# Converting the first two blocks of weights in halves of their rows

## The chip, the cores and the metric

The kernel runs on one core of a Trainium2 chip. The metric is the device time of one execution in microseconds (us); a comparison uses medians of repeated runs. Five engines of the core appear below: PE does the matrix multiplications (PEld is its weight load, which overlaps them), DVE is the vector engine, ACT the scalar engine, POOL takes a little set-up work, and SP issues nearly all transfers between the chip's main memory and on-chip memory. Each engine works through its own instructions in the order in which the program issued them, and waits at an instruction until what it needs is there.

## The reference

A linear attention with decay ("retention") is followed by a two-layer network with a gate. With 4 batches, 8 heads, 768 positions and head size 64:

```python
for t in range(S):
    state = gamma * state + outer(k[:, :, t], v[:, :, t])
    y[:, :, t] = scale * q[:, :, t] @ state
x = y.transpose(0, 2, 1, 3).reshape(3072, 512)
h = x @ w_in                        # 512 x 2048
g = h * erf(softplus(h))
out = g @ w_out                     # 2048 x 512
```

q, k and v are float32. The two weight matrices arrive as float64 and are computed with in float32, so the kernel has to convert them itself.

## The kernel before

**Tiling.** The 3072 token rows are cut into 24 chunks of 128; six chunks make a batch. The retention of a chunk j is a handful of steps: `ret_scale` (DVE scales q and k by their decays), `ret_transpose` (PE transposes, ACT copies to `kT` and `qT`), `ret_scores` (PE, line 445), `ret_mask` (DVE, line 457, writes `am`), `ret_out` (PE: state part at line 485, value part at 492, the new state's part at 501; ACT copies the result into `xT` at line 506) and `ret_add` (DVE adds to `state`, line 619). Four chunks fill one `xT` tile of 512 tokens. The network takes the first 512 tokens with plain products: `hidden(g, u)` makes one block of 128 hidden columns (`ft = 4 g + u`) by four PE matmuls, one for each 128 rows `kk` of `w_in` (line 674), and ACT copies the sum out (line 692); `gate` applies softplus and erf on ACT; `gated` multiplies on DVE (line 661); `project` multiplies with `w_out` (line 710). All later tokens go through `hidden_part` and `project_part` (lines 767 and 839), which use products of sums and differences of blocks, with weights that lie converted on the chip by then.

**Conversion of the weights.** [...] Each piece of weights takes five DVE instructions and one on ACT: line 215 (DVE masks the exponent), 216 (ACT rescales it), 219 and 224 (DVE builds the mantissa), 227 (DVE puts sign and exponent together; this one waits for ACT) and 233 (DVE multiplies the two, into `w_in_sb` or `w_out_sb`). There are 16 pieces (`n` from 0 to 15). Pieces 0 to 3 are converted in two parts of 128 columns each (512 elements a partition), since one part is just one block `ft`: piece 0 makes blocks 0 and 1, piece 1 blocks 2 and 3. Later pieces go whole (1024 elements). Pieces 4 and 5 are the first of `w_out`, 6 and 7 again `w_in`. The raw words of a piece lie in one of four places; the transfer of piece n+4 (`load_pieces_after`, lines 168 and 176, issued by SP) waits until piece n has been read. `conversion` is a generator: `weights()` hands out its steps one at a time, and two things advance it, `need(...)` (run until a block is done) and `pace(...)` (a budget of steps after each piece of other work). So the order of DVE's instructions is fixed when the program is written out, not by what is ready on the chip.

**Around the change.** The first four chunks have an order written out by hand (K_ scale, T transpose, S_ scores, M mask, O_ out, A add). Chunk 2's out step has the transposes of chunk 3's queries put in between; then come the scores of chunk 3, the conversion of block 0, the add of chunk 2, the mask of chunk 3, the conversion of block 1, and the out step of chunk 3:

```python
    O_(2, lambda: T(3, 1))
    S_(3)

    need("in", 0)
    A(2)
    M(3)
    need("in", 1)
    next(weight_steps)
```

Before the out step of chunk 3, PE multiplies block 0 of `w_in` with the 384 tokens of the first three chunks (`first_block`), with three small products of the identity matrix ahead of it (`warm=3`, line 672). Afterwards it does the same for block 1, and then the last 128 tokens of both blocks.

Of the kernel before, what the change touches and what calls it, by code (L numbers as in the profile page):

```python
# [19 lines left out]
P = 128  # L20
C = 128
TCH = 512
# [23 lines left out]
def kernel(  # L46
# [13 lines left out]
    nc = tc.nc  # L60
# [7 lines left out]
    JPC = TCH // C  # L68
# [65 lines left out]
    def w_in_of(ft, kk):  # L134
        half, s, i = ft // (2 * FG), ft % (2 * FG) // FG, ft % FG
        return w_in_sb[:, s, 2 * half + kk // 2, kk % 2, i * P : (i + 1) * P]
# [46 lines left out]
    def load_pieces_after(n):  # L183
        for later in range(n + 1, n_p):
            if place[later] == place[n]:
                load_piece(later)
                break

    def conversion(n):

        which, i = pieces[n]
        half, s, at = i // 4, i % 4 // 2, i % 2

        for part in range(2) if n < 4 else (None,):
            words = raws[place[n]].bitcast(U32)
            if which == "in":
                f = slice(at * 2 * P, (at + 1) * 2 * P)
                if part is not None:  # L200
                    f = slice((at * 2 + part) * P, (at * 2 + part + 1) * P)
                to = w_in_sb[:, s, 2 * half : 2 * half + 2, :, f].rearrange("p d k f -> p (d k) f")
            else:
                to = w_out_sb[:, s, 2 * half : 2 * half + 2, at * 2 : at * 2 + 2, :].rearrange(
                    "p d f c -> p d (f c)"
                )
            words = words.rearrange("p (a b w) -> p a b w", a=to.shape[1], w=2)
            number, power = (
                x.rearrange("p (a b) -> p a b", a=to.shape[1]) for x in (numbers, powers[n % 2])
            )  # L210
            if part is not None:
                f = slice(part * P, (part + 1) * P)
                words, number, power = words[:, :, f], number[:, :, f], power[:, :, f]
            lo, hi = words[:, :, :, 0], words[:, :, :, 1]
            nc.vector.tensor_scalar(power, hi, 0x7FF00000, None, op0=ALU.bitwise_and)
            nc.scalar.activation(power, power, AF.Relu, bias=below, scale=8.0)
            if part is None:
                yield
            nc.vector.tensor_scalar(
                number, hi, 0xFFFFF, 1 << 20, op0=ALU.bitwise_and, op1=ALU.bitwise_or  # L220
            )
            yield
            numberf = number.bitcast(F32)
            nc.vector.scalar_tensor_tensor(numberf, number, 2.0**32, lo, op0=ALU.mult, op1=ALU.add)
            if part is None:
                yield
            nc.vector.scalar_tensor_tensor(
                power, hi, 1 << 31, power, op0=ALU.bitwise_and, op1=ALU.bitwise_or
            )
            if part != 0:  # L230
                load_pieces_after(n)
            yield
            nc.vector.scalar_tensor_tensor(  # L233
                to, numberf, 2.0**-52, power.bitcast(F32), op0=ALU.mult, op1=ALU.mult,
            )
            done.update((which, 2 * i + u) for u in (range(2) if part is None else (part,)))
            yield

    def sums(which, s):
# [14 lines left out]
    done = set()  # L254

    def weights():


        pending = [conversion(n) for n in range(n_p)]
        begun = 0  # L260
        for n, steps in enumerate(pending):
            for k, _ in enumerate(steps, start=begun):
                yield
                if n > 4 and n + 1 < n_p and k == 2:
                    next(pending[n + 1])
                    yield
            begun = int(n > 4)
            if pieces[n] == ("out", 5):
                yield from sums("in", 0)
# [5 lines left out]
    weight_steps = weights()  # L275
# [3 lines left out]
    def pace(n):  # L279

        nonlocal room
        room += n
        while room >= 1:
            next(weight_steps, None)
            room -= 1

    def need(*what):
        nonlocal room
        while what not in done:
            if next(weight_steps, done) is done:  # L290
                next(last_steps)
            room -= 1
# [3 lines left out]
    ident = const.tile([P, P], F32, name="ident")  # L296
# [93 lines left out]
    def ret_psum(pool=None):  # L390

        pool = pool or (next(psum_turn) if early else ps_r)
        return pool.tile([P, HP, C], F32, name="hp" if pool is ps_h else "r")
# [68 lines left out]
    def ret_out(j, between=None, state_last=False):  # L462
        c = j % NC
        m, i = divmod(j, JPC)
        if i == 0:
            XC[m] = ret.tile([P, HP, TCH], F32, name="xT")

        if early:
            pp = [ps_o.tile([P, HP, C], F32, name=f"o{(2 * j + r + 1) % 4}") for r in range(2)]
        else:  # L470
            pp = [ret_psum() for _ in range(2)]

        def place(h):
            return pp[h % 2][h // 4 * D : (h // 4 + 1) * D, h % 4 // 2, :]

        if state_last:
            between()


        if c:  # L480
            for u in PAIRS:
                for r in range(2):
                    h = 2 * u + r
                    own = slice(r * D, (r + 1) * D)
                    nc.tensor.matmul(  # L485
                        place(h), state[own, u, :], QT[j][own, u, :],
                        start=(h % 4 < 2), stop=False, skip_group_check=True,
                    )
        if between is not None and not state_last:
            between()  # L490
        for h in (0, 4, 1, 5, 2, 6, 3, 7):
            nc.tensor.matmul(  # L492
                place(h), V[j][:, h, :], AM[j][:, h % 2, h // 2, :],
                start=(not c and h % 4 < 2), stop=True, skip_group_check=True,
            )

        if c < NC - 1:
            new = SU[j] = pp[0][:, 2:, :].rearrange("p a (b d) -> p (a b) d", d=D)
            for h in range(H):
                r = h % 2  # L500
                nc.tensor.matmul(  # L501
                    new[r * D : (r + 1) * D, h // 2, :], KQ[j][:, 0, h, :], V[j][:, h, :],
                    start=False, stop=True, skip_group_check=True,
                )
        for r in range(2):
            nc.scalar.copy(XC[m][:, r::2, i * C : (i + 1) * C], pp[r][:, :2, :])
        pace(2.5)
# [156 lines left out]

    HP_ = {}

    def hidden_of(ft, t, warm=0):

        if ft not in HP_:
            HP_[ft] = ps_h.tile([P, TCH], F32, name="hp")  # L670
        for _ in range(warm):
            nc.tensor.matmul(HP_[ft][:, :P], ident, ident, start=True, stop=True)
        for kk in range(n_k):
            nc.tensor.matmul(  # L674
                HP_[ft][:, t], w_in_of(ft, kk), XC[0][:, kk, t],
                start=(kk == 0), stop=(kk == n_k - 1),
            )

    def hidden(g, u):
        ft = g * FG + u  # L680
        if u == 0:
            HS[g] = act.tile([P, N], F32, name="h")
        need("in", ft)
        if ft == 0:
            hidden_of(1, slice(TCH - C))
        hidden_of(ft, slice(TCH) if ft > 1 else slice(TCH - C, TCH))

        if ft < FG:
            need("in", ft + 2)
        if ft == 0:  # L690
            ret_add(JPC - 1)
        nc.scalar.copy(HS[g][:, u * TCH : (u + 1) * TCH], HP_.pop(ft))
        done.add(("hidden", ft))
        if ft == FG - 1:
            need("in", FG + 2)
        if g:
            pace_around(3.4 if ft > FG else 0)
# [156 lines left out]
    def put_part(m, step):  # L854
# [27 lines left out]
    K_, T, S_, M, O_, A = (  # L882
        ret_scale, ret_transpose, ret_scores, ret_mask, ret_out, ret_add
    )
# [32 lines left out]
    T(3, 0)  # L917
    A(1)
    K_(3, 1)
    O_(2, lambda: T(3, 1))  # L920
    S_(3)

    need("in", 0)
    A(2)
    M(3)
    need("in", 1)
    next(weight_steps)

    def first_block():
        hidden_of(0, slice(TCH - C), warm=3)  # L930

    ret_out(JPC - 1, first_block, state_last=True)
    early = False
    room = 0.0

# [176 lines left out]
```

## Time and profile before

| | us |
|---|---|
| median of 4 runs | 683.68 (683.57 to 683.94) |
| the profiled execution's own time | 683.66 |
| its span, first to last instruction | 681.9 |
| PE busy | 675.3 |
| DVE busy | 390.5 |
| ACT busy | 256.5 |
| PE busy in the stretch 24.4 to 88.9 us (64.5 us) | 64.48 |
| DVE busy in that stretch | 61.60 |

Some 1.8 us of the profiled execution lie around its span. A row of the timeline gives the start in us, the busy time, the engine, the line of the kernel, the operation, the output and inputs with their shapes, and in brackets how long the engine had been idle just before and what ended that idle time. Timelines merge neighbours of one kind ("x2"), and an instruction may begin a little before the one ahead of it has ended. The chain of waits follows the work that ended last back to what released each step of it; an engine that is not on it at some time had time to spare there. The granted clock of PE is 1.00 in every slice of the profile.

### The profile page before, as it was taken

What the parts mean: (1) busy time and instruction counts of PE and PEld (TensorE: products, weight loads), DVE (VectorE), ACT (ScalarE), POOL (GpSimd) and SP (SyncE); (2) the same over time, 40 slices, a digit from 0 to 9 for tenths busy, and PEclk for the clock granted to TensorE, in tenths of its full rate; (3) what the DMA queues carried; (4) which work ended last, traced back from release to release, by engine and by line L of the source; (5) the groups of instructions that cost most, each with busy time, mean ns of one, the idle gap of its engine ahead of it and who ended that gap; (6) DMA issues with size and microseconds to landing.
All of it is one profiled execution on the core that took longest, in us unless ns stands there. A gap on an engine that the chain in (4) does not pass through costs nothing.

```text
span 681.9 us, 14430 instructions
## 1 busy us (share of the span) xinstructions
PE 675.3 (99%) x6206; PEld 577.2 (85%) x6206; DVE 390.5 (57%) x616; ACT 256.5 (38%) x291; POOL 5.0 (1%) x20
## 2 busy tenths in 40 slices
PE   8999999999999999999999999999999999999998
PEld 7744544577999999999999999999999999999996
DVE  5799999585845634644553564555544554343224
ACT  3367362324414234144144242341441441423431
POOL 1000000100000000000000000000000000000000
PEclk9999999999999999999999999999999999999999
DMA  9999944333412222321321222222312200000000
GB/s 192 220 227 214 229 125 103 63 61 62 116 33 46 75 38 41 75 41 37 78 45 32 64 45 46 67 42 45 71 36 48 59 18 2 1 32 1 1 32 31
DMA packets 156511, 47.64 MB, mean 70 GB/s; under 512 B 143008, under 2 KB 147360, under 8 KB 156448
## 3 DMA queue, kind: packets, MB, share of 16 engines
q1 hardware_dynamic: 156032, 46.72, 31.9%
q8 instruction: 48, 0.79, 0.5%
q14 instruction: 15, 0.12, 0.1%
q10 hardware_dynamic: 416, 0.01, 0.0%
HBM read 40.39 MB, written 6.29 MB: 68 GB/s over the span
## 4 chain that ended last, share of the span: by engine, by line
PE 98%; DVE 0%; ACT 0%; issue 0%; POOL 0%; POOLq 0%
PE hp L767 37%; PE o L839 36%; PE hp L674 8%; PE o L710 8%; PE r L551 1%; PE hp L516 1%; PE o L587 1%; PE r L445 1%; PE o L386 1%; PE hp L566 1%; PE o L492 1%; PE r L432 1%; PE r L566 1%; PE r L492 0%; PE o L485 0%; PE o L501 0%
## 5 line engine op out<-in xcount | busy, mean ns | idle before, releaser
L767 PE MATMUL hp<-xs,w_in_sb 128*128 128x128 f32 x1280 | 149.7, 275 | 0.0
L767 PEld LDWEIGHTS hp<-xs,w_in_sb 128*128 128x128 f32 x1280 | 147.8, 192 | 1.6 <-issue 0.5
L839 PE MATMUL o<-w_out_sb,h 128*128 128x256 f32 x640 | 141.7, 379 | 0.0
L839 PEld LDWEIGHTS o<-w_out_sb,h 128*128 128x128 f32 x640 | 121.6, 190 | 16.5
L767 PE MATMUL hp<-xT,w_in_sb 128*128 128x128 f32 x960 | 113.7, 275 | 0.0
L767 PEld LDWEIGHTS hp<-xT,w_in_sb 128*128 128x128 f32 x960 | 111.9, 192 | 1.9 <-issue 1.0
L839 PE MATMUL o<-w_out_sb,e 128*128 128x256 f32 x480 | 112.1, 383 | 0.0
L661 DVE TENSOR_TENSOR e<-h,e 128x1024 f32<-128x1024 f32 x42 | 49.5, 1220 | 100.0 <-ACT e L642 100.0
L839 PEld LDWEIGHTS o<-w_out_sb,e 128*128 128x128 f32 x480 | 88.2, 190 | 11.6
L674 PE MATMUL hp<-xT,w_in_sb 128*128 128x512 f32 (+2 forms) x144 | 56.8, 548 | 1.0 <-DVE w_in_sb L233 1.0
L792 DVE TENSOR_TENSOR h<-h,hp 128x512 f32<-128x512 f32 x20 | 13.7, 687 | 72.3 <-PE hp L767 72.3
L632 ACT ACT_TABLE_LOAD x24 | 30.8, 1283 | 60.8 <-issue 45.4
L674 PEld LDWEIGHTS hp<-xT,w_in_sb 128*128 128x128 f32 x144 | 25.7, 190 | 27.6 <-issue 25.3
L642 ACT ACTIVATE e<-e 128x2048 f32<-128x2048 f32 (+1 forms) x23 | 42.1, 1836 | 0.2
L632 ACT ACTIVATE e<-h 128x2048 f32<-128x2048 f32 x22 | 42.0, 1910 | 0.2
L780 DVE TENSOR_TENSOR h<-h,hp 128x512 f32<-128x512 f32 x20 | 13.7, 687 | 41.8 <-PE hp L767 41.8
L785 ACT COPY h<-hp 128x512 f32<-128x512 f32 x20 | 11.7, 586 | 61.0 <-PE hp L767 61.0
L790 ACT COPY h<-hp 128x512 f32<-128x512 f32 x20 | 11.7, 585 | 60.3 <-PE hp L767 60.3
L783 ACT COPY h<-hp 128x512 f32<-128x512 f32 x20 | 11.7, 585 | 57.1 <-PE hp L767 57.1
L605 ACT COPY xT<-r 128x256 f32<-128x256 f32 x32 | 10.4, 375 | 54.8 <-PE r L551 54.8
L642 ACT ACT_TABLE_LOAD x24 | 30.8, 1283 | 0.4
L778 ACT COPY h<-hp 128x512 f32<-128x512 f32 x20 | 11.8, 588 | 48.6 <-PE hp L767 48.6
(139 smaller groups left out, 667.1 us busy)
## 6 DMA issues: line engine op xcount, KB each, us to landing
w_out_sb<-in_moe_w_out_dram SPq DMA_DIRECT2D x14, 512.0 KB, 5.4
kq<-in_k_dram SPq DMA_DIRECT2D x23, 256.0 KB, 3.8
v<-in_v_dram SPq DMA_DIRECT2D x23, 256.0 KB, 3.1
out_dram<-r SPq DMA_DIRECT2D x23, 256.0 KB, 3.0
kq<-in_q_dram SPq DMA_DIRECT2D x288, 16.0 KB, 1.8
kb<-in_k_dram SPq DMA_DIRECT2D x288, 16.0 KB, 1.7
w_in_sb<-in_moe_w_in_dram SPq DMA_DIRECT2D x8, 512.0 KB, 12.9
w_out_sb<-in_moe_w_in_dram SPq DMA_DIRECT2D x8, 256.0 KB, 8.4
```

The costliest lines, as they stand in the source:

```text
L566: nc.tensor.matmul(other[a][own, u % 2, D:] if crossed else pp[a][own, u % 2, t], V[j][t, 2 * u + r, :], AM[j][t, r, u, :D], start=crossed ...
L632: nc.scalar.activation(E[g], HS[g], AF.Softplus)
L642: nc.scalar.activation(E[g][:, half], E[g][:, half], AF.Erf)
L661: nc.vector.tensor_tensor(E[g][:, half], HS[g][:, half], E[g][:, half], op=ALU.mult)
L674: nc.tensor.matmul(HP_[ft][:, t], w_in_of(ft, kk), XC[0][:, kk, t], start=(kk == 0), stop=(kk == n_k - 1),)
L710: nc.tensor.matmul(O[0][tt].rearrange("p (d c) -> p d c", d=2), E[g][:, u * TCH + tt * P : u * TCH + (tt + 1) * P], w_out_of(ft), start=(f ...
L767: nc.tensor.matmul(bank[:, u, :], w_in_sb[:, s, IN[a], kk, u * P : (u + 1) * P], XS[m][b][:, kk, :], start=(p in (1, 2, 5) and u == 0 and ...
L778: nc.scalar.copy(h["11"], flat)
L780: nc.vector.tensor_tensor(h["11"], h["11"], flat, op=ALU.add)
L783: nc.scalar.copy(h["12"], flat)
L792: nc.vector.tensor_tensor(h["12"], h["12"], flat, op=ALU.add)
L839: nc.tensor.matmul(O[m][i][:, half, :], G[g][a][:, u * P : (u + 1) * P], w_out_sb[:, s, OUT[b], u, :], start=i not in started, stop=(s == ...
```

## The change

Piece 0, the first of `w_in`, is converted in four steps in place of two: each of its two blocks (0 and 1) is converted first for its rows `kk` 0 and 1 and then for its rows `kk` 2 and 3, so that each of the six instructions handles 256 elements a partition and there are twice as many. The four matmuls of such a block now wait in pairs: those of `kk` 0 and 1 for the first half, those of `kk` 2 and 3 for the second. The first step of block 0's conversion is issued inside chunk 2's out step, right after the transposes of chunk 3's queries. DVE's order does not change by this, but on ACT the exponent step of the first half now stands ahead of the two copies of chunk 2's results to `xT`. One step more was taken ahead of chunk 3's out step before (the beginning of block 2); it is gone there, so on ACT block 2's exponent step now stands behind the copies of chunk 3's results. The three products of the identity matrix ahead of block 0 are gone. From block 3 on the order of the instructions on every engine is as it was.

```diff
@@ -193,7 +193,12 @@
         which, i = pieces[n]
         half, s, at = i // 4, i % 4 // 2, i % 2
 
-        for part in range(2) if n < 4 else (None,):
+
+        parts = itertools.product(
+            range(2) if n < 4 else (None,), (slice(2), slice(2, 4)) if n == 0 else (slice(None),)
+        )
+        for part, rows in parts:
+            last = n > 0 or rows.start == 2
             words = raws[place[n]].bitcast(U32)
             if which == "in":
                 f = slice(at * 2 * P, (at + 1) * 2 * P)
@@ -210,7 +215,8 @@
             )
             if part is not None:
                 f = slice(part * P, (part + 1) * P)
-                words, number, power = words[:, :, f], number[:, :, f], power[:, :, f]
+                words, number, power = words[:, rows, f], number[:, rows, f], power[:, rows, f]
+                to = to[:, rows]
             lo, hi = words[:, :, :, 0], words[:, :, :, 1]
             nc.vector.tensor_scalar(power, hi, 0x7FF00000, None, op0=ALU.bitwise_and)
             nc.scalar.activation(power, power, AF.Relu, bias=below, scale=8.0)
@@ -227,13 +233,14 @@
             nc.vector.scalar_tensor_tensor(
                 power, hi, 1 << 31, power, op0=ALU.bitwise_and, op1=ALU.bitwise_or
             )
-            if part != 0:
+            if part != 0 and last:
                 load_pieces_after(n)
             yield
             nc.vector.scalar_tensor_tensor(
                 to, numberf, 2.0**-52, power.bitcast(F32), op0=ALU.mult, op1=ALU.mult,
             )
-            done.update((which, 2 * i + u) for u in (range(2) if part is None else (part,)))
+            if last:
+                done.update((which, 2 * i + u) for u in (range(2) if part is None else (part,)))
             yield
 
@@ -664,12 +671,10 @@
-    def hidden_of(ft, t, warm=0):
+    def hidden_of(ft, t):
 
         if ft not in HP_:
             HP_[ft] = ps_h.tile([P, TCH], F32, name="hp")
-        for _ in range(warm):
-            nc.tensor.matmul(HP_[ft][:, :P], ident, ident, start=True, stop=True)
         for kk in range(n_k):
             nc.tensor.matmul(
                 HP_[ft][:, t], w_in_of(ft, kk), XC[0][:, kk, t],
@@ -917,19 +922,19 @@
     T(3, 0)
     A(1)
     K_(3, 1)
-    O_(2, lambda: T(3, 1))
+
+    def last_queries():
+        T(3, 1)
+        next(weight_steps)
+
+    O_(2, last_queries)
     S_(3)
 
     need("in", 0)
     A(2)
     M(3)
     need("in", 1)
-    next(weight_steps)
-
-    def first_block():
-        hidden_of(0, slice(TCH - C), warm=3)
-
-    ret_out(JPC - 1, first_block, state_last=True)
+    ret_out(JPC - 1, lambda: hidden_of(0, slice(TCH - C)), state_last=True)
     early = False
     room = 0.0
```

## The prediction

> **What bounds the kernel now.** I read the busy times first, then the chain of waits, then each wait on it. On the page:
>
> ```profile
> PE 675.3 (99%) x6206; PEld 577.2 (85%) x6206; DVE 390.5 (57%) x616; ACT 256.5 (38%) x291; POOL 5.0 (1%) x20
> PE 98%; DVE 0%; ACT 0%; issue 0%; POOL 0%; POOLq 0%
> ```
>
> PE sets the time over the whole, so only a stretch where PE waits can give anything. The chain of waits between 20 and 92 us (start, length, what) shows two such places:
>
> ```profile
> 21.56 0.65 ACT xT L506 x2
> 22.21 0.63 ACT w_out_sb L216
> 22.83 0.02 issue
> 22.86 0.70 DVE w_out_sb L227
> 23.56 0.03 issue
> 23.58 0.70 DVE w_in_sb L233
> 24.28 0.14 issue
> 24.42 2.82 PE hp L674 x8
> ...
> 84.99 3.63 PE hp L674 x8
> 88.62 0.36 PE r L485 x2
> 88.98 0.04 issue
> 89.02 0.66 PE r L485 x14
> ```
>
> The first is what the change works on: ACT copies chunk 2's results, then rescales the exponents of block 0, DVE finishes it, and PE starts at 24.42. The second is easily missed: the 16 records of line 485 take 0.60 us elsewhere on this chain and 1.06 us here, and the four matmuls ahead of them show 3.63 in place of 3.44. PEld's waits from 84 to 90 us say why:
>
> ```profile
> PEld r L485 <- DVE am L457: 1.0, 2, 0.8
> ```
>
> Line 485 of chunk 5 writes into the banks from which DVE still reads chunk 5's scores, so PE stands still until DVE has made the masks: (1.06 - 0.60) + (3.63 - 3.44) = 0.65 us. What holds DVE before that? Its timeline (brackets: idle time ahead and what ended it):
>
> ```profile
> 34.27 0.69 DVE L227 SCALAR_TENSOR_TENSOR w_in_sb<-w_out_sb,w_in_sb 128x512 uint32<-128x512 uint32 x1 [1.28 <-ACT w_in_sb L216]
> 47.93 0.69 DVE L215 TENSOR_SCALAR w_out_sb<-w_out_sb 128x1024 uint32<-128x1024 uint32 x1
> 58.18 0.69 DVE L215 TENSOR_SCALAR w_out_sb<-w_in_sb 128x1024 uint32<-128x1024 uint32 x1 [0.29 <-DMA w_in_sb<-in_moe_w_in_dram]
> ...
> 87.68 1.28 DVE L457 TENSOR_TENSOR am<-r,causal 128x512 f32<-128x512 f32 x2
> ```
>
> At 58.18 DVE waits for a transfer (piece 6). From there to 140 us its list of waits holds only that one and one at the far end:
>
> ```profile
> DVE h L780 <- PE hp L767: 7.7, 1, 7.7
> DVE w_out_sb L215 <- DMA w_in_sb<-in_moe_w_in_dram: 0.3, 1, 0.3
> ```
>
> So from 58.18 to the masks' end at 87.68 + 1.28 = 88.96 DVE runs without a wait, at its own speed, and PE cannot pass 89.02 before it. One more landing matters. SP's transfers of piece 4 (line 176, issued at 38.77 and 39.69) have these times to landing:
>
> ```profile
> DMA to landing us min/median/max: 5.1/6.6/8.1
> ```
>
> The second lands at 39.69 + 8.1 = 47.8, and DVE's first instruction on it starts at 47.93: just on time, without a recorded wait. At the other landing, piece 6's second half (issued at 42.78, 15.3 us to landing), DVE starts 0.09 us after.
>
> **The change, step by step.** All against the profiled execution: 683.66 us, a span of 681.9 and 1.8 around it; it lies 0.02 under the median of the runs, 683.68.
>
> *Prices of the halves.* No row of before shows a 256-element conversion step. Line 215 takes 0.42 with 512 elements and 0.69 with 1024, so a half is 0.42 - 0.27/2 = 0.28 (bounds: 0.21, half of it; 0.42, no shorter). Lines 224, 227 and 233 take 0.69 and 1.23, so a half is 0.42, which is also what the 128x256 add at line 619 shows (0.41). ACT's line 216 takes 0.72 and 1.15, a half 0.51 (bounds 0.375, the 128x256 copy of line 605; 0.72). Independent DVE steps begin 0.07 before the last has ended, dependent ones 0.03 after. A half then takes 1.69 us from start to start on DVE, a block 3.38 against 2.73 (25.72 to 28.44): 0.65 more for each of two blocks.
>
> [...] The rows of lines 215 and 224 hold a fixed 0.15 us an instruction (0.42 - 0.27). [...]
>
> *Block 0.* Line 215 starts at 20.91 as before (its transfer sets that). First half on DVE: 20.91, 21.11, 21.43; ACT rescales 21.22 to 21.73, without the copies ahead of it; line 227 at 21.78 no longer waits (0.46 before); line 233 ends at 22.65. With the 0.14 us handover PE starts at 22.79 instead of 24.42. ACT's copies of chunk 2, moved behind, run 21.66 to 22.31 instead of 21.56 to 22.21: in time for 22.79. Second half: line 233 ends at 24.32, PE's second pair at 24.46, after the first pair ended at 22.79 + 1.41 = 24.20: a new wait of 0.26. The block ends at 25.87 instead of 27.24: PE leads by 1.37. The identity products (0.94 us, 22.53 to 23.47) lay inside the wait, so their removal itself gains nothing.
>
> *Chunk 3 and block 1.* Behind the halves DVE adds the state (24.25 to 24.66) and masks (to 25.87); PE needs them at 25.87 and 26.47. Block 1's halves are done at 27.53 and 29.20; PE comes at 27.96 and needs the second pair at 29.37. ACT's copies of chunk 3 end at 28.85, needed at 30.8. The lead stays 1.37. DVE is 0.68 late here (29.12 against 28.44).
>
> *Blocks 2 and 3.* Block 2 is ready at 32.07, needed by PE at 32.6. In block 3 DVE waited 1.28 us for line 216 because ACT stood at block 0's copy (33.03) waiting for PE. With PE 1.37 ahead that copy starts at 31.66, ACT is done at 33.4, and DVE goes through at 33.59 instead of 34.27: late by 0.68 becomes early by 0.68.
>
> *Where the lead goes.* At 47.93 DVE may come 0.7 to 0.85 early (another 0.17 of ACT waiting at 46.59 goes too), but piece 4 lands at 47.8: it keeps 0.03. ACT's erf (51.11) stands behind DVE's first step on piece 4, so it does not move, nor does the copy of chunk 4's queries behind it (ends at 54.47); PE, which took them at 55.41, would arrive at 54.04, waits until about 54.5 and keeps 0.9. At 58.18 piece 6 holds DVE: lead 0.00. The landings do not follow DVE: SP issued both transfers by 42.8, from a queue held back by earlier landings, and the wait of SP for DVE before piece 7's (47.31) comes after them. So the masks still end at 88.96; PE arrives 0.9 earlier, and waits 0.65 + 0.9 = 1.55 us there instead of 0.65.
>
> *Sum.* -1.37 at block 0, +0.47 at chunk 4's scores, +0.90 at chunk 5's masks: 0.0. After 89.02 all engines find what they found before. Forecast 683.6.
>
> *Bounds.* With both upper prices (0.42 and 0.72) a block takes 3.92, DVE is 1.8 late after block 1, 0.55 after the vanished 1.28, 0.4 at 47.93, and 0.1 after the 0.29 at 58.18: 683.8. With the lower prices DVE is only earlier at waits that stay: 683.6. The landings may shift a little; the runs' spread of 0.37 bounds that.
>
> **The rivals.**
>
> *The lead survives (faster).* If the two landings came 1.5 us earlier, or DVE did not gate chunk 5, PE would keep its lead: 683.66 - 0.9 = 682.8 to 683.66 - 1.37 = 682.3. For it: PE is on 98% of the chain, and its wait at 24.4 really goes. Against it: DVE has no idle time between 58.18 and 88.96 to give up. If only part of it (0.1 to 0.6) survives, the time is 683.1 to 683.5, inside 0.2%.
>
> *DVE becomes late (slower).* If a half costs as much as a whole on DVE, a block takes 5.46: DVE is 5.0 late after block 1; the 1.28, the 0.17 and the 0.29 take back 1.7, and some 3.2 reach the masks at 88.96, all paid by PE: 686.9. The point from which it decides is a DVE later than 58.1 at piece 6. Against it: line 619's 0.41 for 256 elements.
>
> *The change does nothing at its own place*: if ACT's first half waited as long as before, PE would start near 24.4 as before and the end would also be 683.7; it differs in the trace alone.
>
> **How the numbers follow.** About 0.2% (1.4 us) is what a measurement of this kernel can tell from no change. Lead fully lost or nearly (the forecast, with the partial case and the no-effect case): 0.84, 683.1 to 683.9. Lead survives: 0.11, at 682.3 to 682.8, of which some lie inside 0.2% (over 682.3), so 0.07 counts as faster and 0.04 as the same. DVE late: 0.05. Faster 0.07, same 0.88, slower 0.05. The range goes from 682.7, into the surviving lead, to 684.0, the upper price and the runs' spread.
>
> **What would show it.** Right: line 233's first half ends near 22.7 and PE's block 0 starts near 22.8; block 0 ends near 25.9; no DVE wait for ACT in block 3; a DVE wait of 0.6 us or more for a transfer near 47.9, and 0.3 again at 58.2; PEld's wait for the masks grows from 1.0 to about 1.9 us; the masks end at 88.9 to 89.0. Wrong: piece 6's first step before 57.9, or masks before 88.5 (then the lead is partly kept), or piece 4's first step after 48 (then DVE is late).

## The result and the profile after

The changed kernel takes 682.54 us (median of 38 runs, 682.16 to 683.47) against 683.65 us before (58 runs, nearly all from 683.35 to 684.28): a ratio of 0.9984, 95% interval 0.9979 to 0.9988. That is 1.1 us less, inside the 0.2% that the prediction called "the same", though the interval excludes 1, and 0.16 us below the range of 682.7 to 684.0. The profiled execution of the changed kernel took 682.96 us, a span of 681.3; it lies 0.42 above the median, which matters below.

The page of the changed kernel, busy times and the chain of waits by engine:

```profile
PE 674.8 (99%) x6200; PEld 576.1 (85%) x6200; DVE 391.1 (57%) x626; ACT 257.2 (38%) x293; POOL 5.5 (1%) x20
...
PE 86%; DVE 7%; issue 2%; SPq 2%; ACT 1%; DMA 1%; ACTq 0%; DVEq 0%
```

Before, PE held 98% of the chain. Now the chain leaves PE at chunk 5's masks and goes back along DVE to the first landing of weights. Its two ends, between 20 and 26 us and between 86 and 92 us (start, length, what):

```profile
13.66 7.53 DMA w_out_sb<-in_moe_w_in_dram
21.19 0.03 issue
21.22 0.02 DVEq L221
21.24 0.05 issue
21.29 0.29 DVE w_out_sb L221
...
22.24 0.35 DVE w_out_sb L233
22.59 0.02 issue
22.62 0.42 DVE w_in_sb L239
...
87.00 1.29 DVE am L464 x2
88.29 0.04 issue
88.33 0.66 PE r L492 x14
88.99 1.02 PE r L499 x16
```

(Lines 215, 227, 233, 457, 485 and 492 of before are 221, 233, 239, 464, 492 and 499 here.) Where ACT's copies of chunk 2 stood before, there is now nothing but the landing and DVE's five short steps. At the other end DVE's masks hold PE: the profile's list of PEld's waits from 84 to 90 us has this line (us in total, times, longest).

```profile
PEld r L492 <- DVE am L464: 1.3, 2, 0.9
```

It was 1.0 before. PE's timeline of the changed kernel (brackets: idle time ahead, and what ended it) gives the places that the prediction put numbers on:

```profile
23.19 3.13 PE L679 MATMUL hp<-xT,w_in_sb 128*128 128x384 f32 x8 [0.42 <-DVE w_in_sb L239]
26.25 0.67 PE L492 MATMUL o<-qT,state 64*64 64x128 f32 x16
...
54.42 1.16 PE L452 MATMUL r<-qT,kT 64*128 64x128 f32 x16
...
87.74 0.43 PE L492 MATMUL r<-qT,state 64*64 64x128 f32 x2
88.33 0.66 PE L492 MATMUL r<-qT,state 64*64 64x128 f32 x14 [0.17 <-DVE am L464]
88.92 1.09 PE L499 MATMUL r<-am,v 128*64 128x128 f32 x16
```

And DVE's timeline at the places shown of before:

```profile
33.93 0.69 DVE L233 SCALAR_TENSOR_TENSOR w_in_sb<-w_out_sb,w_in_sb 128x512 uint32<-128x512 uint32 x1
...
47.60 0.69 DVE L221 TENSOR_SCALAR w_out_sb<-w_out_sb 128x1024 uint32<-128x1024 uint32 x1
...
57.48 0.67 DVE L221 TENSOR_SCALAR w_out_sb<-w_in_sb 128x1024 uint32<-128x1024 uint32 x1
...
87.00 1.28 DVE L464 TENSOR_TENSOR am<-r,causal 128x512 f32<-128x512 f32 x2
```

None of the four has a bracket. The wait of 1.28 us for ACT at block 3 is gone, as forecast; the wait for piece 6 (58.18 before, 57.48 now) is gone too, and none has come at piece 4 (47.60). DVE's whole list of waits from 22 to 140 us:

```profile
DVE h L785 <- PE hp L772: 7.8, 1, 7.8
DVE e L668 <- ACT e L649: 0.2, 1, 0.2
DVE w_in_sb L233 <- ACT w_in_sb L222: 0.2, 1, 0.2
```

**Where the time went.** Between the two profiles, PE starts on block 0 1.23 us earlier (24.42 to 23.19). It loses 0.31 between the block's halves (3.13 in place of 2.82), so it starts the state products 0.92 earlier (27.17 to 26.25). At chunk 4's scores it is still 0.92 ahead (54.42 against the line of before below): nothing was given back there.

```profile
55.34 1.16 PE L445 MATMUL r<-qT,kT 64*128 64x128 f32 x16
```

At chunk 5's masks it loses 0.24, and starts chunk 5's value products 0.68 earlier (89.61 to 88.93). The execution is 0.70 shorter, 683.66 to 682.96. The other 0.4 of the difference of medians is not between these two profiles, because the profiled execution of the changed kernel is 0.42 slower than that kernel's median; the experiments show what an execution's time hangs on.

### The profile page after: what moved, and what is told of

It is laid out like the page before. It is cut to its first block, busy times and chain, and to the rows that moved or that the text cites. A ratio compares the mean times of both kernels' runs of the same rounds, so it can differ in the third digit from the quotient of the medians.

```text
span 681.3 us, 14431 instructions
## 1 busy us (share of the span) xinstructions
PE 674.8 (99%) x6200; PEld 576.1 (85%) x6200; DVE 391.1 (57%) x626; ACT 257.2 (38%) x293; POOL 5.5 (1%) x20
## 4 chain that ended last, share of the span: by engine, by line
PE 86%; DVE 7%; issue 2%; SPq 2%; ACT 1%; DMA 1%; ACTq 0%; DVEq 0%
PE hp L772 37%; PE o L844 36%; PE o L715 6%; PE hp L679 2%; PE r L558 1%; PE hp L523 1%; SPq L118 1%; DMA w_out_sb<-in_moe_w_in_dram 1%; DVE w_out_sb L230 1%; PE o L594 1%; DVE w_out_sb L225 1%; DVE w_in_sb L233 1%; DVE w_out_sb L233 1%; DVE w_out_sb L221 1%; PE hp L573 1%
```

## The experiments

The expectations set theories against each other by letters. Theory A keeps the prediction's gates: the landings of pieces 4 and 6 hold DVE in every execution. Theory B says that the landings held DVE in one execution by chance, and that DVE's own work, from the first landing to chunk 5's masks, sets the time. Where a further letter appears, the expectation says what it stands for. Five numbers of each profile are used throughout: L, the landing of the first piece of weights; D, the start of DVE's first conversion step (0.09 behind L); S, PE's start on block 0; M, the end of chunk 5's masks on DVE; V, PE's start on chunk 5's value products. "Piece 6" is the landing of its second half. Values read from different views can differ by 0.01.

| kernel profiled (all in us) | L | S | M | V | piece 6 | time |
|---|---|---|---|---|---|---|
| before (first profile) | 20.82 | 24.42 | 88.96 | 89.61 | 58.09 | 683.66 |
| before again | 21.74 | 24.80 | 89.08 | 89.72 | 56.45 | 683.77 |
| changed | 21.20 | 23.19 | 88.28 | 88.93 | 54.55 | 682.96 |
| changed again | 21.10 | 23.10 | 88.20 | 88.85 | 53.80 | 682.88 |
| one DVE step earlier in before | 21.23 | 24.73 | 88.70 | 89.46 | 55.33 | 683.50 |
| extra DVE work in changed | 21.35 | 23.34 | 89.79 | 90.44 | 55.68 | 684.50 |
| halves alone | 21.48 | 24.26 | 89.34 | 89.98 | 55.82 | 684.03 |
| move alone | 20.60 | 23.66 | 87.82 | 88.47 | 53.98 | 682.52 |
| early masks in changed | 20.87 | 22.87 | 85.94 | 87.90 | 54.38 | 681.98 |
| early masks in before | 20.81 | 24.91 | 87.12 | 89.63 | 56.86 | 683.69 |
| no identity products in before | 21.72 | 24.98 | 90.83 | 91.48 | 56.79 | 685.52 |
| late first piece in changed | 21.61 | 23.61 | 88.73 | 89.38 | 54.71 | 683.42 |
| late first piece in before | 21.24 | 24.55 | 88.78 | 89.42 | 55.06 | 683.47 |
| early piece and early masks | 19.46 | 22.84 | 85.61 | 87.59 | 55.00 | 681.64 |

Time minus V is 594.03 to 594.08 us in every row: what these kernels change has no effect behind V, so the whole case lies ahead of it. Two paths end at V. DVE's gives V = M + 0.65 wherever PE waits for the masks. PE's, where it doesn't wait, gives V = S + 64.72 with whole blocks (89.46 - 24.73 with one DVE step earlier in before, 89.63 - 24.91 with early masks in before) and S + 65.03 with the 0.31 between the halves (87.90 - 22.87, early masks in changed). The later of the two sets the time.

### Both kernels once more

No edit.

> The kernel before, unchanged, once more with a profile: do the landings that held the vector engine in the first profile repeat? Theory A (the forecast's step: the landings of pieces 4 and 6 hold DVE, and the change itself made them earlier): piece 4's second half lands at 47.8 and piece 6's at 58.1 again, within 0.3 us, with a DVE wait of about 0.3 us at 58.2. Theory B (how late they land changes from execution to execution and has nothing to do with the change): they land elsewhere, by 1 us or more, and DVE's wait at 58.2 is gone or larger. Both: the time is 683.4 to 684.0, and PE waits for chunk 5's masks near 88.6 to 89.0.

> The changed kernel, unchanged, once more with a profile. Theory A: the landings are at 45.9 and 54.6 again, within 0.3 us. Theory B: they are elsewhere by 1 us or more; where piece 6 lands later than 57.4 DVE waits for it and the masks end later by just that. Both: 682.2 to 683.4; PE waits about 0.9 us for the masks of chunk 5.

Before took 683.77 us. Its piece 6 landed at 56.45 instead of 58.09, piece 4 at 46.37 instead of 47.81, and DVE waits for neither. DVE's list of waits from 23 to 140 us, before once more:

```profile
DVE h L780 <- PE hp L767: 7.8, 1, 7.8
DVE w_in_sb L227 <- ACT w_in_sb L216: 1.4, 2, 1.2
DVE e L661 <- ACT e L642: 0.2, 1, 0.2
```

The wait for block 3 is there again (1.2), the wait for piece 6 is not, and the time is the same within 0.11 us. DVE came to piece 6 at the same time as in the first profile (58.18), now without a bracket:

```profile
58.17 0.69 DVE L215 TENSOR_SCALAR w_out_sb<-w_in_sb 128x1024 uint32<-128x1024 uint32 x1
```

So the gate that the prediction rests on is not a property of the kernel before: theory A falls. Of the 14 profiles in the table, the first one of before has the latest piece 6, and it alone has a DVE wait for a landing of piece 4 or 6.

The changed kernel again: 682.88, and M - D = 67.01 us (66.99 in its first profile). DVE runs from the first landing to the masks with next to no idle time, so the time of the changed kernel should follow L: time minus L is 661.76 and 661.78, with L 0.10 apart; the late landing below tests it further. By this the median, 682.54, would belong to a landing near an estimated 20.8 (682.54 - 661.77), which no profile of this kernel shows. In before it is 662.84 and 662.03: there block 0 does not hang on the landing alone. In the first profile DVE stood 0.46 us for ACT there; in the second, with the landing 0.92 later, it did not stand for ACT at all.

### One DVE step earlier, the rest as before

If DVE decides, taking away its wait of 1.28 us at block 3 should help without any of the change. In before, one step of conversion is issued ahead of block 0's copy on ACT, so that ACT rescales block 3 in time:

```diff
             ret_add(JPC - 1)
+            next(weight_steps)
         nc.scalar.copy(HS[g][:, u * TCH : (u + 1) * TCH], HP_.pop(ft))
```

> The kernel before with one step more of the conversion ahead of block 0's copy on ACT, so that block 3's exponent step does not stand behind that copy: DVE's 1.28 us of waiting at 34.3 goes, PE's start on block 0 stays at 24.4. Theory B (the end is set by when DVE comes to chunk 5's masks): DVE leads by 1.3 at the masks, PE's stall of 0.65 there goes: 683.65 - 0.65 = 683.0. Theory A (landings hold DVE): 683.65, within 0.1. Theory C (PE's earlier start on block 0 is itself the gain): 683.65.

It took 683.66 us against 683.72, ratio 1.0, 0.9991 to 1.0008: nothing. DVE's list of waits from 22 to 140 us:

```profile
DVE h L781 <- PE hp L768: 7.8, 1, 7.8
DVE w_in_sb L227 <- ACT w_in_sb L216: 1.0, 2, 0.6
DVE w_out_sb L227 <- ACT w_out_sb L216: 0.5, 2, 0.4
DVE e L661 <- ACT e L642: 0.2, 1, 0.2
```

The wait at block 3 is gone, but 1.13 us of it came back at later blocks (0.17 at 38.95, 0.61 at 42.39, 0.35 at 46.70), each for ACT, whose conversion step stands behind its copy of a block that PE had not finished. DVE can't run ahead of PE in this stretch: ACT's copies tie it to PE's pace. PE's own path ended at S + 64.72 = 89.45, with S at 24.73 as late as in before. Theory B's 683.0 was a miss, since it left out the second path (the table has DVE's masks 0.26 earlier than in the first profile of before, and V only 0.15). To gain, a change must move both: PE's start and DVE's masks.

### Extra work on DVE in the changed kernel

Two adds of 128x512 into a tile that nothing reads, behind block 3:

```diff
             need("in", ft + 2)
+        if ft == 1:
+            same = ident[:, None, :].to_broadcast([P, 4, P])
+            for _ in range(2):
+                nc.vector.tensor_tensor(junk, same, same, op=ALU.add)
         if ft == 0:
```

> The changed kernel with two extra DVE instructions of 512 elements behind block 3's conversion, some 1.25 us of work that nothing uses; PE's start on block 0 stays at its new place. Theory B: DVE's lead of 1.07 at the masks is used up: 682.54 + 1.25 - 0.0 to 0.3 = 683.5 to 683.8. Theory A: part of the work hides behind the landings: 682.6 to 683.0. Theory C: PE's lead of 1.37 stays: 682.5.

The result is 684.5 us (683.68 to 684.85), ratio 1.0011 to before, 1.0002 to 1.002. The two adds and what follows them on DVE's timeline:

```profile
35.43 1.41 DVE L699 TENSOR_TENSOR junk<-ident 128x512 f32<-128x512 f32 x2
36.76 0.42 DVE L221 TENSOR_SCALAR w_out_sb<-w_in_sb 128x512 uint32<-128x512 uint32 x1
```

They delay DVE by 1.33 us. M - D grows from 67.0 to 68.35, and V - L from 67.73 to 69.09: the whole delay reaches V, 50 us later, and with it the end. No landing took any of it up, and PE found no slack. In the changed kernel DVE decides, as theory B says. Per landing the price is 1.36 us; against the profile of changed it is 684.50 - 682.96 = 1.54, and the medians differ by 1.96. The rest of that, 0.6 us, is not accounted for by the added work, and with it the result lies 0.7 above the expected 683.5 to 683.8; the landings of the unprofiled executions are not known.

### Chunk 5's masks earlier, in both kernels

The same edit in both takes the masks of chunk 5 ahead of two of DVE's conversion instructions (lines 225 and 230, in before 219 and 224), which take 1.9 us:

```diff
-            ([(T, 5)], []),
-            ([(S_, 5), (M, 5)], []),
+            ([(T, 5), (pace, -1.5)], []),
+            ([(S_, 5), (M, 5), (pace, 1.5)], []),
```

> The changed kernel with chunk 5's masks two DVE instructions (1.87 us) earlier; the two conversion steps they pass come right behind them. Theory B/D (the end is set by when DVE has made these masks; PE stands 0.9 us at them in both profiles of the changed kernel): that stall goes and the lead of 1.37 us arrives whole: 682.5 - 0.9 = 681.6. Theory C (PE's start alone counts, the masks do not): no change, 682.5. If PE meets another wait behind the masks that is as late, 682.5 too, and the trace shows which.

> The kernel before with chunk 5's masks two DVE instructions earlier. Theory B/D: PE's stall there, 0.65 us in one profile of before and 0.27 in the other, goes: 683.7 - 0.3 to 0.65 = 683.05 to 683.4. Theory C: 683.7.

In the changed kernel: 681.98 us (681.76 to 682.51), ratio to before 0.9977, 0.9968 to 0.9986. In before: 683.64, ratio 1.0, 0.9991 to 1.0008. PE's timeline at chunk 5's state products, of changed with early masks:

```profile
83.67 3.70 PE L679 MATMUL hp<-xT,w_in_sb 128*128 128x512 f32 x8
87.30 0.67 PE L492 MATMUL r<-qT,state 64*64 64x128 f32 x16
87.89 1.09 PE L499 MATMUL r<-am,v 128*64 128x128 f32 x16
```

The sixteen records stand together in 0.67 us, without a bracket: the wait for the masks is gone, and V lies at S + 65.03. Per landing, V moved from L + 67.73 to L + 67.03, 0.70 earlier; the medians differ by 0.56. The 0.9 that was expected is what PEld's list showed for the longest wait; PE itself stood only 0.71 beyond its own path (88.93 - 23.19 - 65.03). In before the same edit frees PE in the same manner and gains nothing, where theory B expected 0.3 to 0.65: PE started at 24.91, and 24.91 + 64.72 = 89.63 is as late as the V of before (89.61 and 89.72). There the masks cost PE 0.47 us in the first profile and 0.20 in the second, and in the execution with early masks PE's start was later than in both and set V. So PE's lead was real, and part of it was lost at the masks.

### The two parts of the change by themselves

The halves alone, with ACT's order and the identity products of before (only the removed and restored lines are shown):

```diff
-    def last_queries():
-        T(3, 1)
-        next(weight_steps)
-
-    O_(2, last_queries)
+    O_(2, lambda: T(3, 1))
...
-    ret_out(JPC - 1, lambda: hidden_of(0, slice(TCH - C)), state_last=True)
+    next(weight_steps)
+
+    def first_block():
+        hidden_of(0, slice(TCH - C), warm=3)
+
+    ret_out(JPC - 1, first_block, state_last=True)
```

> Only the halves: block 0's and 1's conversion in halves, but the first exponent step behind the copies of chunk 2's results, block 2's exponent step ahead of the copies of chunk 3's, and the identity products kept. ACT is then done with the first half near 22.6, PE starts near 23.7 and block 0 ends near 26.7 instead of 27.24. Theory D (the lead of PE on block 0 arrives through block 0's copy on ACT, which lets block 3's exponent step and so DVE through): lead 0.5, 683.7 - 0.5 = 683.2. Theory A (landings): 683.7.

And the move alone: before with its whole blocks, and block 0's first step ahead of the copies of chunk 2:

```diff
-    O_(2, lambda: T(3, 1))
+
+    def last_queries():
+        T(3, 1)
+        next(weight_steps)
+
+    O_(2, last_queries)
```

> Only the move: block 0's exponent step whole, ahead of the copies of chunk 2's results; no halves, identity products kept, block 2's step where it was. DVE's wait of 0.46 for ACT goes, PE starts near 23.9 instead of 24.42. Theory D: lead 0.45 (less where the first transfer lands late), 683.7 - 0.45 = 683.25. Theory A: 683.7.

The halves alone: 683.89 us, ratio 1.0006, 0.9997 to 1.0015, no gain and perhaps a small loss. One of its eleven executions took 685.56. DVE's timeline there:

```profile
23.22 0.43 DVE L233 SCALAR_TENSOR_TENSOR w_out_sb<-w_out_sb 128x256 uint32<-128x256 uint32 x1 [0.69 <-ACT w_out_sb L222]
```

DVE still waits for ACT, which copies chunk 2 first, and the halves add their own work on top: M - D is 67.77, and PE waits 1.2 us at the masks in its list. The expected 683.2 was a miss: PE started at 24.26, 0.2 and 0.5 earlier than in the profiles of before, but the masks ended at 89.34, later than in both, and V is M + 0.65.

The move alone: 682.97 us (682.52 to 683.52), ratio 0.999, 0.9981 to 0.9999. ACT's timeline there:

```profile
21.15 0.72 ACT L216 ACTIVATE w_out_sb<-w_out_sb,below 128x512 uint32<-128x512 uint32 x1 [0.28 <-DVE w_out_sb L215]
21.78 0.63 ACT L506 COPY xT<-o 128x256 f32<-128x256 f32 x2
```

One ACT instruction ahead of two copies gives 0.6 us of the 1.1, more than the 0.45 that was expected. It serves both paths: PE starts 0.8 to 1.1 us earlier than in the two profiles of before (with a landing, 20.60, earlier than in either), and at block 0 DVE doesn't stand at line 227. Per landing, V is L + 67.87, against L + 67.73 with the whole change, so the halves add 0.14 us by the profiles and 0.43 by the medians (which were not measured side by side, and whose landings are unknown). By either number the move is the larger part of the gain; how much the halves add is not settled more closely.

### Before without the identity products

```diff
     def first_block():
-        hidden_of(0, slice(TCH - C), warm=3)
+        hidden_of(0, slice(TCH - C))
```

> The kernel before without the three identity products ahead of block 0, nothing else. The forecast priced their removal at nothing, since they lie in PE's wait: 683.65, within 0.1, PE's start on block 0 unmoved and its eight records still 2.8 us. Rival: an idle PE is slower afterwards, then block 0's records take longer and the time grows.

The median is 683.82 us, ratio 1.0004, 0.9995 to 1.0013, but two of the ten executions took 685.52 and 685.21; the other eight lie from 683.46 to 684.02. The profiled one is the slowest. Block 0 on its PE timeline:

```profile
24.97 4.51 PE L674 MATMUL hp<-xT,w_in_sb 128*128 128x384 f32 x8 [1.82 <-DVE w_in_sb L233]
```

And PE alone in stretches of 1 us (length, PE busy and records, granted clock, DMA's share, GB/s):

```profile
24.00:25.00 1.00, 0.03 (x1) 1.00 1.10 222
25.00:26.00 1.00, 1.00 (x3) 0.70 1.13 228
26.00:27.00 1.00, 1.00 (x3) 0.50 1.12 227
27.00:28.00 1.00, 1.00 (x3) 0.50 1.15 235
28.00:29.00 1.00, 1.00 (x4) 0.59 1.13 231
29.00:30.00 1.00, 1.00 (x18) 1.00 1.12 222
```

Behind 1.82 us without a matmul the granted clock was 0.50 for an estimated 3.4 us (0.60, 1.00, 1.00 and 0.82 of the four slices from 25 to 29, if it was 1.00 in the rest of them), and the block took 4.51 us instead of 2.82: 1.69 us, which reaches the end (24.98 + 64.72 + 1.69 = 91.39; V is 91.48, which is M + 0.65, since DVE was late as well). With the three products, 0.95 and 1.23 us of the gap are left in the two profiles of before, where the clock stays at 1.00. The products do not exclude such times: two of the 58 executions of before (685.47 and 685.73) and one of the eleven of the halves alone (685.56) have them too, but none of these three was profiled, and none of the 82 executions of before that ran beside the experiments is over 684.12. In the changed kernel the gap is 0.42 us without the products, its clock stays at 1.00, and none of its 38 executions is over 683.5. That taking them out costs nothing there fits the prediction; that the short gap is the reason is argued, since no run puts the products back into the changed kernel.

### The first landing later, in both kernels

If the changed kernel follows L one for one and before doesn't, then moving the first transfer of weights behind one transfer of values must cost the one and not the other:

```diff
         load_values(j - 1)
-    load_piece(0, 0)
     load_values(JPC - 1)
+    load_piece(0, 0)
     load_piece(0, 1)
```

> The changed kernel with the second half of the transfer of block 0's raw words... that is, both of its transfers, issued behind chunk 3's values instead of ahead of them, so block 0's words land some 1.1 us later. Theory E (in the changed kernel DVE never stops between this landing and chunk 5's masks, so the time is the landing plus a constant; 661.77 in both profiles of it): 682.54 + 1.1 = 683.6 to 683.7. If the masks were not the end of that chain, or another transfer held DVE: less than +0.5.

> The same order of transfers in the kernel before. There ACT's copies of chunk 2's results end at 22.2 to 22.5 whatever the landing is, and block 3's step waits for PE, so a landing of 20.8 has about 0.6 us to spare: 683.65 + 0.3 to 0.5 = 683.9 to 684.2. If before also goes with the landing: +1.1, 684.75.

Changed: 683.42 us (682.93 to 683.99; 683.6 to 683.7 had been expected), 0.9 over its own median of 682.54 and nearly all of its gain lost: ratio to before 0.9997, 0.9988 to 1.0006. Before: 683.68 against 683.70, no change, where 0.3 to 0.5 had been expected. In the profile of changed, time minus L is 661.81, as in its two other profiles. That the edit moved the landing in every execution is not shown: L is 0.4 to 0.5 later than in the two profiles of changed (1.1 had been expected), and in before, at 21.24, it lies between the landings of its two profiles, so for before the test rests on the medians. That before does not follow L one for one its two profiles show as well: L 0.92 apart, the times 0.11. Its block 0 hangs on ACT's copies of chunk 2 too: in the profile with the late piece DVE still stood 0.16 us for ACT at line 227, so the landing could have come later by that much. The change took these copies off the path, and what is left on it is the landing.

### A version faster than both

The same two facts point to the next step: let piece 0 come earlier, and take the masks out of PE's way. To the changed kernel with early masks, one line moves the first transfer ahead of chunk 2's values:

```diff
         load(j)
+        if j == JPC - 1:
+            load_piece(0, 0)
         load_values(j - 1)
-    load_piece(0, 0)
     load_values(JPC - 1)
```

> The changed kernel with chunk 5's masks two instructions earlier, as before, and with block 0's transfers issued ahead of chunk 2's values, so that they land near 19.7. PE then no longer waits for block 0: it can start when chunk 3's scores are done (22.5 instead of 22.86) and the gap of 0.3 between the halves closes: 681.98 - 0.5 to 0.65 = 681.3 to 681.5. If chunk 2's values, now behind, hold PE by more than 0.5 us: 682.0 or above.

681.68 us (681.60 to 681.95), ratio to before 0.997, 0.9958 to 0.9981: 2.0 us less than before, 0.9 less than changed, and 0.2 above the expected 681.3 to 681.5. L is 19.46, and PE starts on block 0 right behind chunk 3's scores. PE's and then DVE's timeline at block 0:

```profile
22.84 2.85 PE L680 MATMUL hp<-xT,w_in_sb 128*128 128x384 f32 x8
25.61 0.67 PE L493 MATMUL o<-qT,state 64*64 64x128 f32 x16
```

```profile
21.44 0.43 DVE L233 SCALAR_TENSOR_TENSOR w_out_sb<-w_out_sb 128x256 uint32<-128x256 uint32 x1 [0.94 <-ACT w_out_sb L222]
```

No bracket ahead of 22.84, and 2.85 us for the block: the wait between the halves has gone as well. V - S is 64.75, PE's path without a stop. DVE has 0.94 us to spare at line 233, where it waits for ACT behind the copy of chunk 3's queries. So in this execution the landing no longer sets the time. That its six executions spread over 0.35 us, and the 38 of changed over 1.3, fits.

## Why the prediction was wrong

**What bounds the kernel: right, but half of it.** PE's wait at block 0 and the wait at chunk 5's masks were the right two places. That the masks stood in PE's way was read correctly, but its 0.65 us was 0.46: the other 0.19, the 3.63 us of the four matmuls ahead, was no wait. The changed kernel with early masks has the same 3.63 us on its chain and no wait behind it:

```profile
83.74 3.63 PE hp L679 x8
87.37 0.60 PE r L492 x16
```

That a change must move both paths to V is shown by the runs that move only one (one DVE step earlier, early masks in before, halves alone: three times nothing).

**Prices of the halves: right.** 0.28 to 0.29 for lines 221 and 225, 0.42 to 0.43 for the others, 0.51 on ACT, as worked out. Block 1 takes DVE 3.32 us from start to start (26.15 to 29.47, before 25.72 to 28.44): 0.60 more, where 0.65 was forecast. By the rows here the busy times of the block grow by 0.75 (0.15 for each of five extra instructions), and the overlap of neighbours takes off 0.15.

**Block 0: right.** From D, PE was to start after 1.88 us and the state products after 4.96. Measured: 23.19 - 21.29 = 1.90 and 26.25 - 21.29 = 4.96; the wait between the halves was 0.31, forecast 0.26. The landing came 0.38 later than in the profile before, so the times themselves are 0.4 higher than the numbers in the text.

**Blocks 1 to 3: right.** Line 233 of block 3 was to start 12.68 us after D without a wait: 33.93 - 21.29 = 12.64, and the 1.28 us have gone. DVE was 0.65 late behind block 1, forecast 0.68.

**"Where the lead goes": wrong, and with it the sum.** The step says that DVE, early by 0.7 to 0.85 at piece 4, is held there to 0.03 and at piece 6 to 0.00 by landings at 47.8 and 58.1. In the changed kernel piece 4 landed at 45.95 and 45.41, piece 6 at 54.55 and 53.80, and DVE never waited for them. From D to the masks' start DVE took 87.68 - 20.91 = 66.77 us before and 87.00 - 21.29 = 65.71 after, 1.06 less: +0.65 in blocks 0 and 1, -1.37 up to block 3's line 233, -0.36 up to piece 6 (the wait of 0.29 among it), +0.02 behind it. Where the text has 0.00 for DVE, it is 1.06, of which 0.38 went to the later landing of that execution. The size belongs to this pair of profiles: in the second pair the same stretch takes 65.96 and 65.72 us, only 0.24 apart, because DVE's first step of before came 0.92 later there and then stood less. The masks' end came earlier in both pairs, by 0.68 and 0.88. "The landings may shift a little; the runs' spread of 0.37 bounds that" was the mis-sized bound: before's times don't show how landings spread, since nothing in before but that one wait of 0.29 was seen to hang on them. Over the profiles here piece 4 landed from 45.2 to 47.8 and piece 6 from 53.8 to 58.1. The text took two times out of one execution, the latest of 14, for fixed ones.

**Chunk 4's scores: wrong.** +0.47 was to be lost there to ACT's chain behind DVE's first step on piece 4. With DVE early, ACT's erf and the copies moved too (the copy of chunk 4's queries starts at 53.54 instead of 53.87), and PE, which came with a lead of 0.92 and not 1.37, kept it.

**Chunk 5's masks: right place, wrong size.** PE was to lose 0.90 there. It lost 0.24 between the two profiles, since the masks came 0.68 earlier; beyond PE's own path, it waits 0.47 in the one and 0.71 in the other. The extra work (all of it passed on) and the early masks (0.70 gained per landing) show that DVE sets the end there.

**The rivals.** "The lead survives" has the measured time, 682.54, inside its 682.3 to 682.8, but its account holds only in part: between the profiles 0.68 of PE's 0.92 reached V, and DVE did gate chunk 5. The first of its two conditions was "the two landings came 1.5 us earlier": in the 13 other profiles piece 4 landed 1.2 to 2.6 us earlier and piece 6 1.2 to 4.3, those of before among them. It was argued against with "DVE has no idle time between 58.18 and 88.96 to give up", which is true and is no argument: DVE's lead had been won before 58.18, and no landing took it away. "DVE becomes late" did not happen in the changed kernel: DVE was at piece 6 at 57.48, 0.6 ahead of its point of 58.1. With the halves alone it came there at 58.54, past that point, and V was 0.3 to 0.4 later than in before.

**Signs.** The text named "piece 6's first step before 57.9, or masks before 88.5" as what would show it wrong. Both came: 57.48 and 88.28.

**What stays open.** Why the landings of one and the same program differ from execution to execution: SP issues the transfers of pieces 4 and 6 within 2.2 us of the same time in all profiles, and piece 6 lands up to 4.3 us apart. It is also open whether the change itself makes them earlier: piece 6 landed from 53.80 to 55.68 in the six profiles with the whole change, and from 55.06 to 58.09 in the six with neither its halves nor its move. No run here tells. In the profile of changed DVE came to piece 6 at 57.48, so a landing at 58.09 would have held it there by an estimated 0.7 us (58.18 - 57.48).

## What to carry to other kernels

A wait for a transfer that one profile shows is a gate only if a second profile shows it too (the 0.29 us at piece 6 stand in one of 14); look at the same row in two executions before a forecast lets it swallow a gain. Where two engines meet again later (here PE and DVE at one chunk's masks), follow both paths to the meeting point: a change that shortened one alone gave nothing here. An instruction that stands behind copies on a third engine can serve both at once when it is moved (0.6 of the 1.1 us here), and what then sets the time is what was hidden behind those copies, here a landing that could be moved as well.

## What the runs showed of the hardware

Two things were not expected. Without the identity products, in the profiled execution of before, the granted clock of PE was 0.50 for an estimated 3.4 us behind a gap of 1.82 us without a matmul, where it had been 1.00, and the eight matmuls of block 0 took 4.51 us instead of 2.82; a second of its ten executions, not profiled, has a like time (685.21), and the other eight have not, so it is not sure to happen. Whether the executions of 685.47 to 685.73 us in kernels that keep the products are the same is not known.

And landings move by 0.9 to 1.6 us between two executions of one program whose times differ by 0.11 us: the first piece of weights from 20.82 to 21.74 in before, piece 6 from 58.09 to 56.45. The changed kernel, whose path hangs on such a landing, seems to show it as spread: with the first piece late, eleven executions each spread over 1.06 us in changed and 0.43 in before. Their landings were not profiled.
